# Key, value, wo and w2 loads issued from GpSimd with each engine's eight rows framed as one packet, landings relayed by the sync engine

## The chip, the cores and the metric

The kernel runs on one core of one Trainium2 chip. Its time is device microseconds of one execution of the program, here the median of several runs; a separate view of it is the profile, which records one execution instruction by instruction. The core has five engines that run their own instruction streams: TensorE (PE, with its weight loads shown as PEld), VectorE (DVE), ScalarE (ACT), GpSimd (POOL) and SyncE (SP), which computes nothing and issues transfers. Transfers between the chip's memory and the core's SBUF run on 16 DMA engines. Engines and transfers are ordered by semaphores alone.

## What is computed

One step of decoding for one token, with float32 throughout. A row x of 512 numbers is normalized; the result goes through an attention over a stored cache and through a two-layer MLP, and both are added to x:

```python
xn = _layernorm(x)                             # (1, 1, 512)
q  = (xn @ wq)                                 # 32 query heads of 128
scores = einsum(q, k) * 128 ** -0.5            # 8 key/value heads, 65536 positions, 4 queries a head
o  = softmax(scores) @ v
y  = x + o @ wo + maximum(xn @ w1, 0) @ w2     # w1: 512 x 1792, w2: 1792 x 512
```

The keys and the values are 256 MB each; wq and wo are 8 MB each, w1 and w2 3.5 MB each. Every byte is used once.

## The kernel before

All key/value heads are laid out one behind the other as 524288 positions, cut into `NCH` = 32 chunks of 16384 positions, four to a head. A chunk of keys is 8 MB and fills the tile `kt`, 128 partitions with 64 KB each; a chunk of values fills `vt` in the same way. There is one buffer of each. While keys arrive in `kt`, the values in `vt` are used, and the other way round. A third large tile, `wt`, holds w1 at first and w2 at the end. `kt` holds wq before the first keys and wo after the last.

**Who loads.** SP issues every load, in an order written out by hand: wq in three pieces (L151, L159), w1 (L160), then in turn a chunk of keys and a chunk of values (L162 to L169), then wo in three pieces (L173), w2 in five (L177) and the store of the result (L179). All go to one queue, so each DMA engine works them off in that order. Before a load into a tile that is in use, SP waits for a semaphore that says that the tile is free: `kfree` for `kt`, `vfree` for `vt`. `take` (L50) is this wait; it lowers the semaphore again. A landed load adds 16 to its own semaphore, `k` or `v`, for which PE waits in the same way (L308, L287). A partition's row of a load, 64 KB of a chunk, is one contiguous piece; an engine gets eight rows of the 128.

**What a chunk goes through.** When a chunk of keys has landed, PE multiplies it with the queries (L313) into PSUM in eight rounds, and DVE transposes the scores into the tile `tr` (L366). DVE takes the maximum (L384 to L391), and ACT computes the correction for the running maximum (L254), which adds to `kfree`, and then the exponentials (L256). When the values of the chunk have landed, PE multiplies them with the exponentials (L292); the matmul behind that (L299) adds to `vfree`. PE's loop, the block "turns", does in each turn the values of the chunk before and the keys of the next one.

**What GpSimd does.** It prepares constants (L191 to L206), the end of the normalization (L208 to L214), and then the first layer of the MLP: it waits for w1 (L217), scales w1 in place by the normalized row in four instructions (L219) and adds the four parts in three (L222 to L224). The last of them adds to `sum`, on which PE waits at L286 in the first turn that has values, ahead of those values, to add up the partitions (L281, three times, only the last of which is read). At the very end GpSimd applies the maximum with zero (L226, tile `hT`) when DVE has transposed the sums (L404, semaphore `hx`).

**The first and the last part.** wq is used like a chunk of keys with the normalized row as the query. A DVE instruction near its end, the `nop` at L365, adds to `kfree`, and the first keys may come. At the end PE multiplies wo with the heads' outputs (L313 again), w2 with `hT` (L331, L339), DVE turns the result into one row per partition (L417), and SP stores it.

Of the kernel before, what the change touches and what calls it, by code (L numbers as in the profile page):

```python
# [13 lines left out]
D = 512  # L14
# [21 lines left out]
NCH = SK // CHUNK  # L36
# [6 lines left out]
WO_CUTS = [16, 8, 8]  # L43
W2_CUTS = [6, 4, 2, 1, 1]
# [5 lines left out]
def take(e, sem, n=1):  # L50

    return e.sem_inc(sem, -n).wait_op(sem, n, "sem-ge")  # L52


def starts(cuts):
    return [sum(cuts[:i]) for i in range(len(cuts) + 1)]

# [2 lines left out]
def attention_and_mlp_kernel(  # L60
# [12 lines left out]
    sp, pe, dve, act, pool = nc.sync, nc.tensor, nc.vector, nc.scalar, nc.gpsimd  # L73
    scale = float(DH) ** -0.5

    def sbuf(name, *shape):
        return nc.alloc_sbuf_tensor(name, list(shape), F32).ap()
# [3 lines left out]
    def sem(name):  # L81
        if name not in sems:
            sems[name] = nc.alloc_semaphore(name)
        return sems[name]

    def after(ins, name, n=1):

        return ins.wait_op(sem(name), n, "sem-ge")

    kt = sbuf("kt", P, CHUNK)  # L90
    vt = sbuf("vt", P, CHUNK)
    wt = sbuf("wt", P, FB * D)
# [20 lines left out]
    hT = sbuf("hT", P, FB)  # L113
# [25 lines left out]
    wo_row = wo[0].rearrange("d j n -> d (j n)")  # L139
    w1_row = w1.rearrange("p a f -> p (a f)")  # L140
    w2_row = w2.rearrange("p b n -> p (b n)")
    v_row = v[0].rearrange("(n p b) d -> n p (b d)", p=P, b=NB)
    wq_at, wo_at, w2_at = starts(WQ_CUTS), starts(WO_CUTS), starts(W2_CUTS)

    def of_own_row(cols, groups):
# [11 lines left out]
    for i in range(1, len(WQ_CUTS)):  # L157
        cut = slice(wq_at[i], wq_at[i + 1])
        sp.dma_start(kt[:, cut], wq_row[:, cut]).then_inc(sem(WQ_SEMS[i]), 16)  # L159
    sp.dma_start(wt, w1_row).then_inc(sem("w1"), 16)  # L160
    take(sp, sem("kfree"))
    sp.dma_start(kt, k[0, 0]).then_inc(sem("k"), 16)  # L162
    with sp.Fori(0, NCH - 1) as n:
        take(sp, sem("vfree"))
        sp.dma_start(vt, v_row[bass.ds(n, 1)].rearrange("o p n -> (o p) n")).then_inc(sem("v"), 16)
        take(sp, sem("kfree"))
        sp.dma_start(kt, k[0, bass.ds(n + 1, 1)].rearrange("o p n -> (o p) n")).then_inc(sem("k"), 16)
    take(sp, sem("vfree"))
    sp.dma_start(vt, v_row[NCH - 1]).then_inc(sem("v"), 16)  # L169
    take(sp, sem("kfree"))  # L170
    for i in range(len(WO_CUTS)):
        cut = slice(wo_at[i] * D, wo_at[i + 1] * D)
        sp.dma_start(kt[:, cut], wo_row[:, cut]).then_inc(sem(f"wo{i}" if i else "k"), 16)  # L173
    sp.wait_ge(sem("hT"), 1)
    for i in range(len(W2_CUTS)):
        cut = slice(w2_at[i] * D, w2_at[i + 1] * D)
        sp.dma_start(wt[:, cut], w2_row[:, cut]).then_inc(sem(f"w2{i}"), 16)  # L177
    sp.wait_ge(sem("y"), 1)
    sp.dma_start(out.rearrange("(p a) -> p a", p=P), ysb[:, 0, :]).then_inc(sem("ends"), 16)  # L179

# [3 lines left out]
    def link(ins):  # L184

        if chain[0]:
            after(ins, "pool", chain[0])
        chain[0] += 1
        return ins.then_inc(sem("pool"), 1)
# [22 lines left out]
    link(pool.tensor_scalar_mul(xn, xc, st[:, 7:8]))  # L212
    take(pool, sem("ends"), 16)
    after(pool.tensor_copy(qpad[:, :XA], xn), "pool", chain[0]).then_inc(sem("q"), 1)  # L214
    f = DFF_ALL
    w1_of = [wt[:, a * f : (a + 1) * f] for a in range(XA)]
    pool.wait_ge(sem("w1"), 16)  # L217
# [2 lines left out]
    last.then_inc(sem("pool"), 1)  # L220
    chain[0] += 1
    after(pool.tensor_add(w1_of[0], w1_of[0], w1_of[1]), "pool", chain[0])  # L222
    link(pool.tensor_add(w1_of[2], w1_of[2], w1_of[3]))  # L223
    after(pool.tensor_add(w1_of[0], w1_of[0], w1_of[2]), "pool", chain[0]).then_inc(sem("sum"), 1)  # L224
    hbig = ysum[:, : FB * 32].rearrange("p (b i) -> p b i", i=32)
    after(pool.tensor_scalar_max(hT, hbig[:, :, 0], 0.0), "hx").then_inc(sem("hT"), 1)  # L226


    def next_of(ins):
# [41 lines left out]
    with nc.body("turns", valid_engines=[pe.engine]):  # L271
# [3 lines left out]
        with pe.If(t > 1):  # L275
# [12 lines left out]
            n = NB // WIDE  # L288
# [167 lines left out]
```

## Time and profile before

| | |
|---|---|
| time, median of 3 runs | 1303.71 us (1303.1 to 1303.74) |
| span of the profiled execution, from its first to its last instruction | 1301.3 us |
| what lies around the span, by the median | 2.4 us |
| keys: issue to landing, median of 32 | 24.1 us |
| values: issue to landing, median of 32 | 29.3 us |
| mean granted TensorE clock | 0.755 |

The profile's page shows the busy time of each engine, the span in 40 slices with the busy tenths of each engine and of the 16 DMA engines, the DMA queues with their packets, the chain of work that ended last, and the costliest groups of instructions with the idle time before them and what ended it. In a group, `out<-in` names the tiles, `x32` is the number of instructions, and L313 is line 313 of the kernel. In the timeline a row begins with its start and its duration in us; SPq and POOLq are the parts of SP and GpSimd that issue transfers and handle semaphores. A row of the busy time by windows gives the window, its length, the busy time of PE, PEld, DVE, ACT and POOL in it with the number of instructions, the granted TensorE clock, the mean busy share of the DMA engines, and GB/s.

### The profile page before, as it was taken

The numbers are of one execution on the slowest core, as the hardware profiler recorded it, in microseconds if no ns is written. First come the engines' busy times: TensorE is split into PE (matmuls) and PEld (weight loads), VectorE is DVE, ScalarE is ACT, GpSimd is POOL, SyncE is SP. The second block draws the span as 40 slices with busy tenths as digits, with TensorE's granted clock in tenths as the row PEclk, the third lists the DMA queues.
The fourth block names the chain that finished last, engine by engine and source line by source line (L and its number), as shares of the span: only waits on it lengthen the run. The fifth ranks groups of instructions, "written<-read, shape, count | busy, mean of one in ns | idle before, by whom it ended". The sixth has DMA issues, their size and how long they took to land.

```text
span 1301.3 us, 13055 instructions
## 1 busy us (share of the span) xinstructions
PE 774.9 (60%) x5474; PEld 231.1 (18%) x5474; DVE 274.8 (21%) x466; ACT 76.2 (6%) x299; POOL 34.8 (3%) x30
## 2 busy tenths in 40 slices
PE   3365674665576456566555566666567466557557
PEld 1111121111121111121111121111112111112112
DVE  2211222211222220222220122221122221122222
ACT  1000000000000000000000000000000000000000
POOL 1900000000000000000000000000000000000000
PEclk9677877776887777786776777677777777777779
DMA  9999999999999999999999999999999999999998
GB/s 403 451 419 451 419 451 419 435 435 419 451 419 451 419 451 419 449 421 423 447 419 451 419 451 419 451 419 435 435 419 451 419 451 419 451 419 443 427 420 370
DMA packets 11236, 561.02 MB, mean 431 GB/s; under 512 B 1505, under 2 KB 1505, under 8 KB 1890
## 3 DMA queue, kind: packets, MB, share of 16 engines
q1 hardware_dynamic: 11088, 561.00, 99.7%
q10 hardware_dynamic: 146, 0.00, 0.0%
q8 instruction: 1, 0.02, 0.0%
q14 instruction: 1, 0.01, 0.0%
HBM read 560.99 MB, written 0.00 MB: 431 GB/s over the span
## 4 chain that ended last, share of the span: by engine, by line
issue 94%; DMA 3%; POOL 2%; SPq 0%; PE 0%; DVE 0%; POOLq 0%
DMA wt<-w 3%; POOL wt L219 1%; POOL wt L224 0%; POOL wt L222 0%; POOL wt L223 0%; SPq L177 0%; SPq L159 0%; PE banks L339 0%; DVE ysb L417 0%; SPq L151 0%; POOL hT L226 0%; SPq L452 0%; POOLq L156 0%
## 5 line engine op out<-in xcount | busy, mean ns | idle before, releaser
L313 PE MATMUL banks<-kt,qpad 128*32 128x512 f32 x2176 | 310.0, 733 | 311.1 <-PEq L52 308.7
L292 PE MATMUL banks<-vt,probs 128*16 128x512 f32 x2048 | 271.3, 690 | 82.1 <-PEq L52 82.1
L366 DVE STREAM_TRANSPOSE tr<-banks 128x1024 f32<-128x1024 f32 x136 | 170.0, 1250 | 471.4 <-PE banks L313 466.8
L313 PEld LDWEIGHTS banks<-kt,qpad 128*32 128x32 f32 x2176 | 84.5, 131 | 509.6 <-issue 496.3
L281 PE MATMUL banks<-wt,ones 128*1 128x448 f32 x768 | 121.3, 786 | 0.0
L292 PEld LDWEIGHTS banks<-vt,probs 128*16 128x16 f32 x2048 | 68.4, 108 | 298.4 <-issue 298.4
L392 DVE COPY o_sb<-banks 128x512 f32<-128x512 f32 x32 | 22.1, 692 | 455.3 <-PE banks L292 455.3
L254 ACT ACTIVATE corr<-diff 128x8 f32<-128x8 f32 x32 | 6.7, 208 | 1179.8 <-ACTq L52 1179.8
L256 ACT ACTIVATE probs<-tr,nb_new 128x128 f32<-128x128 f32 x128 | 65.3, 521 | 0.0
L276 PE MATMUL banks<-ident,m 128*4 128x128 f32 x32 | 9.7, 303 | 78.9 <-DVE m L384 78.9
L302 PE MATMUL banks<-sel,o_sb 128*128 128x4 f32 x256 | 32.8, 252 | 18.7 <-PEq L52 18.7
L302 PEld LDWEIGHTS banks<-sel,o_sb 128*128 128x128 f32 x256 | 31.0, 191 | 20.6 <-issue 20.6
L226 POOL TENSOR_SCALAR hT<-ysum 128x14 f32<-128x14 f32 x1 | 0.3, 257 | 1220.7 <-DVE ysum L404 1220.7
L384 DVE TENSOR_REDUCE m<-tr 128x4 f32<-128x512 f32 x32 | 32.2, 1006 | 2.9
L281 PEld LDWEIGHTS banks<-wt,ones 128*1 128x1 f32 x768 | 20.2, 100 | 58.9 <-issue 58.4
L277 PE MATMUL banks<-dg,ones 4*128 4x4 f32 x64 | 15.4, 309 | 20.0 <-DVE dg L387 20.0
L256 ACT ACTIVATION_READ_ACCUMULATOR probs<-tr,nb_new 128x1 f32 x128 | 24.0, 187 | 0.0
L276 PEld LDWEIGHTS banks<-ident,m 128*4 128x4 f32 x32 | 2.6, 81 | 108.0 <-DVE m L384 108.0
L219 POOL TENSOR_SCALAR wt<-wt,xn 128x1792 f32<-128x1792 f32 x4 | 19.1, 4797 | 16.5 <-DMA wt<-w 16.5
L277 PEld LDWEIGHTS banks<-dg,ones 4*128 4x128 f32 x64 | 12.6, 245 | 27.1 <-DVE dg L387 27.1
L299 PEld LDWEIGHTS banks<-part_sum,ones 128*128 128x128 f32 x64 | 9.5, 188 | 27.2 <-issue 27.2
L395 DVE TENSOR_TENSOR lo_run<-lo_run,banks 128x8 f32<-128x8 f32 x32 | 5.2, 163 | 40.0 <-DVEq L52 40.0
(69 smaller groups left out, 91.1 us busy)
## 6 DMA issues: line engine op xcount, KB each, us to landing
kt<-wq SPq DMA_DIRECT2D x2, 2048.0 KB, 9.3
kt<-wq SPq DMA_DIRECT2D x1, 4096.0 KB, 20.8
kt<-wo SPq DMA_DIRECT2D x1, 4096.0 KB, 15.5
kt<-wo SPq DMA_DIRECT2D x2, 2048.0 KB, 22.2
wt<-w SPq DMA_DIRECT2D x1, 3584.0 KB, 28.9
wt<-w SPq DMA_DIRECT2D x1, 1536.0 KB, 9.5
wt<-w SPq DMA_DIRECT2D x1, 1024.0 KB, 11.7
kt<-k SPq DMA_DIRECT2D x32, 24.1
```

The lines of the kernel that those rows point to most:

```text
L219: last = pool.tensor_scalar_mul(w1_of[a], w1_of[a], xn[:, a : a + 1])
L256: last = act.activation(probs[:, :, g], tr[:, :, g], AF.Exp, bias=nb_new[:, g : g + 1], scale=scale, accum_out=part_sum[:, g : g + 1],)
L276: after(pe.transpose(pma[:GROUP, :P], m, ident), "d2p").then_inc(sem("p2d"), 1)
L277: after(pe.matmul(pmb[:, :GROUP], ones[:GROUP, :], dg, start=True, stop=True), "d2p", 2).then_inc(sem("p2d"), 1)
L281: ins = pe.matmul(hrow[32 * c : 32 * c + 1, :], ones[:, :1], hb[:, :, 32 * c : 32 * c + 32], start=True, stop=True,)
L292: last = pe.matmul(acc[c : c + WIDE * GROUP, :], probs[:, b : b + WIDE, :].rearrange("p b g -> p (b g)"), vt[:, b * DH : (b + WIDE) * DH], ...
L299: pe.matmul(lo_new[:, 0, :], ones, part_sum, start=True, stop=True).then_inc(sem("vfree"), 1)
L302: last = pe.matmul(lo_new[:, 1, :], o_sb[:, b, :], sel[:, b, :], start=(b == 0), stop=(b == WIDE - 1),)
L313: last = pe.matmul(pair[s // 2 % 2][32 * c : 32 * c + 32, s % 2 * 512 : s % 2 * 512 + 512], qpad, kb[:, s * 16 : s * 16 + 16, c, :], start ...
L366: ins = after(dve.transpose(tr2[:, s * 1024 : (s + 1) * 1024], pair[s % 2]), "p2d", s + 1)
L384: dve.reduce_max(m, tr.rearrange("p b i -> p i b")[:, :GROUP, :], axis=AX.X).then_inc(sem("d2p"), 1)
L392: after(dve.tensor_copy(o_sb.rearrange("p b d -> p (b d)"), acc), "p2d", 7).then_inc(sem("d2p"), 1)
```

## The change

Five things are done.

- SP no longer issues keys, values, wo and w2. GpSimd does, in `load_keys`, `load_values` and two loops, each with the same wait for `kfree`, `vfree` or `hT` as before. GpSimd has a queue of its own for them; wq, w1 and the store stay on SP's.
- Each of these loads, but for the first chunk of keys, is issued with `single_packet=True`: the eight rows that a DMA engine gets of it are framed as one packet.
- The landings of keys and values count up two new semaphores, `k_in` and `v_in`, which nothing lowers. SP waits for each landing in turn and adds 16 to `k` or `v` (`relay`), on which PE waits as before. The first piece of wo is passed on in the same way.
- The first keys and the first values are issued by GpSimd between its copy of the normalized row (L214) and its wait for w1 (L217). The second chunk of keys and all that follow stand behind its work on w1 (L224).
- w2 is issued by GpSimd behind its own instruction that writes `hT`.

```diff
+def relay_of(sem):
+
+    def relay(e, to, of, n):
+        e.sem_inc(sem(to), 16).wait_op(sem(of), n, "sem-ge")
+
+    return relay
...
-    take(sp, sem("kfree"))
-    sp.dma_start(kt, k[0, 0]).then_inc(sem("k"), 16)
-    with sp.Fori(0, NCH - 1) as n:
-        take(sp, sem("vfree"))
-        sp.dma_start(vt, v_row[bass.ds(n, 1)].rearrange("o p n -> (o p) n")).then_inc(sem("v"), 16)
-        take(sp, sem("kfree"))
-        sp.dma_start(kt, k[0, bass.ds(n + 1, 1)].rearrange("o p n -> (o p) n")).then_inc(sem("k"), 16)
-    take(sp, sem("vfree"))
-    sp.dma_start(vt, v_row[NCH - 1]).then_inc(sem("v"), 16)
-    take(sp, sem("kfree"))
-    for i in range(len(WO_CUTS)):
-        cut = slice(wo_at[i] * D, wo_at[i + 1] * D)
-        sp.dma_start(kt[:, cut], wo_row[:, cut]).then_inc(sem(f"wo{i}" if i else "k"), 16)
-    sp.wait_ge(sem("hT"), 1)
-    for i in range(len(W2_CUTS)):
-        cut = slice(w2_at[i] * D, w2_at[i + 1] * D)
-        sp.dma_start(wt[:, cut], w2_row[:, cut]).then_inc(sem(f"w2{i}"), 16)
+    for n in range(NCH):
+        relay(sp, "k", "k_in", 16 * (n + 1))
+        relay(sp, "v", "v_in", 16 * (n + 1))
+    relay(sp, "k", "wo0", 16)
     sp.wait_ge(sem("y"), 1)
...
     after(pool.tensor_copy(qpad[:, :XA], xn), "pool", chain[0]).then_inc(sem("q"), 1)
+    def load_keys(n, **how):
+        take(pool, sem("kfree"))
+        pool.dma_start(kt, k[0, n], **how).then_inc(sem("k_in"), 16)
+
+    def load_values(n):
+        take(pool, sem("vfree"))
+        pool.dma_start(vt, v_row[n], single_packet=True).then_inc(sem("v_in"), 16)
+
+    load_keys(0)
+    load_values(0)
...
     after(pool.tensor_add(w1_of[0], w1_of[0], w1_of[2]), "pool", chain[0]).then_inc(sem("sum"), 1)
+    for n in range(1, NCH):
+        load_keys(n, single_packet=True)
+        load_values(n)
+    take(pool, sem("kfree"))
+    for i in range(len(WO_CUTS)):
+        cut = slice(wo_at[i] * D, wo_at[i + 1] * D)
+        pool.dma_start(kt[:, cut], wo_row[:, cut], single_packet=True).then_inc(sem(f"wo{i}"), 16)
     hbig = ysum[:, : FB * 32].rearrange("p (b i) -> p b i", i=32)
     after(pool.tensor_scalar_max(hT, hbig[:, :, 0], 0.0), "hx").then_inc(sem("hT"), 1)
+    pool.wait_ge(sem("hT"), 1)
+    for i in range(len(W2_CUTS)):
+        cut = slice(w2_at[i] * D, w2_at[i + 1] * D)
+        pool.dma_start(wt[:, cut], w2_row[:, cut], single_packet=True).then_inc(sem(f"w2{i}"), 16)
```

More of the change, by code (lines that the diff above doesn't have):

```diff
@@ L88, in after @@
         return ins.wait_op(sem(name), n, "sem-ge")
+    relay = relay_of(sem)
     kt = sbuf("kt", P, CHUNK)
```

## The prediction

> **What bounds the kernel now.** I read the page from the top: the span, the busy shares, the DMA row of the 40 slices, the queues, the chain.
>
> ```profile
> span 1301.3 us, 13055 instructions
> PE 774.9 (60%) x5474; PEld 231.1 (18%) x5474; DVE 274.8 (21%) x466; ACT 76.2 (6%) x299; POOL 34.8 (3%) x30
> ...
> DMA  9999999999999999999999999999999999999998
> GB/s 403 451 419 451 419 451 419 435 435 419 451 419 451 419 451 419 449 421 423 447 419 451 419 451 419 451 419 435 435 419 451 419 451 419 451 419 443 427 420 370
> DMA packets 11236, 561.02 MB, mean 431 GB/s; under 512 B 1505, under 2 KB 1505, under 8 KB 1890
> ...
> q1 hardware_dynamic: 11088, 561.00, 99.7%
> ...
> issue 94%; DMA 3%; POOL 2%; SPq 0%; PE 0%; DVE 0%; POOLq 0%
> ```
>
> No engine is busy over 60%, while the 16 DMA engines are at nine tenths or more in every slice but the last. The chain calls 94% "issue" because it cannot follow a semaphore loop back to a transfer, so the DMA row decides: all 561 MB come through SP's queue q1. The 11088 packets of q1 are 9856 rows (128 for each of 64 key and value loads, 3 of wq, 1 of w1, 3 of wo, 5 of w2, and the store) and 16 semaphore writes for each of these 77 transfers (1232): **every row is a packet of its own.**
>
> Does a gap or the rate make the 1301 us? In the busy time by windows the last two columns are the DMA share and GB/s, and a packet is booked where it starts. Narrow windows therefore give the duration of one packet (share x width x 16 engines), and windows around a burst give the cadence.
>
> ```profile
> 608.42:608.43 0.01, 0.01 (x4) 0.00 (x0) 0.00 (x0) 0.01 (x1) 0.00 (x0) 0.50 15.12 6554
> 1284.36:1284.38 0.02, 0.02 (x4) 0.00 (x0) 0.00 (x0) 0.00 (x0) 0.00 (x0) 1.00 1.91 819
> 1292.54:1292.56 0.02, 0.00 (x0) 0.00 (x0) 0.02 (x1) 0.00 (x0) 0.00 (x0) 1.00 0.97 410
> 1294.66:1294.68 0.02, 0.02 (x3) 0.02 (x1) 0.00 (x0) 0.00 (x0) 0.00 (x0) 1.00 0.50 205
> ```
>
> ```profile
> 610.83:611.21 0.38, 0.15 (x4) 0.00 (x0) 0.00 (x0) 0.00 (x0) 0.00 (x0) 0.50 6.39 2760
> 1249.38:1249.87 0.49, 0.00 (x0) 0.00 (x0) 0.00 (x0) 0.00 (x0) 0.00 (x0) 0.50 4.96 2140
> ```
>
> The first row is one packet of 64 KB (6554 GB/s x 0.01 us): 15.12 x 0.01 x 16 = 2.419 us. The others are 16, 8 and 4 KB: 0.611, 0.310 and 0.160 us. The second pair each hold 16 rows of 64 KB, the first row on each engine of the key load issued at 607.56 and of the last value load, 33 loads on: (1249.62 - 611.02) / 33 = 19.35 us a load, which is 8 x 2.419. So there is **no gap between loads**: 64 x 19.35 = 1238 us of the span are packets end to end. The durations are a straight line plus a constant: from 4 to 64 KB, (2.419 - 0.160) / 60 = 0.03765 us per KB, so 64 KB are 2.410 us and 9 ns are left over; 16 KB gives 8.5 ns, 8 KB 9 ns. Each row costs **9 ns beside its bytes**. That, and the start and the end, is all that an issue can win.
>
> **The change, part by part.** *Framing.* 31 key loads (the first is not framed), 32 value loads, 3 of wo and 5 of w2 become one packet per engine: 71 loads with seven packet ends fewer each. The trace has no packet of several rows. If the 9 ns go with the packet, 7 x 9 = 63 ns a load and 71 x 63 ns = 4.5 us go; if they go with the row, nothing; the bytes alone set 2.410 us a row, so more cannot go and nothing in these rows makes it a loss. I take 4.5: in every row above the constant comes with one packet end, from 4 to 64 KB alike.
>
> By the Trainium skill (DMA: Bandwidth & Descriptors, Why small descriptors are slow) a packet costs about 3 cycles inside the engine, joining descriptors saves only that and is "only worth it at ≤256 B desc size", which speaks against this change. At that page's 850 MHz that is 3.5 ns of the 9 measured, by estimate 71 x 7 x 3.5 ns = 1.7 us.
>
> *Issue from GpSimd in the stream.* A load must have its first packet ready when the one before it ends.
>
> ```profile
> 607.56 0.33 SPq L167 DMA_DIRECT2D kt<-k  x1
> 621.20 0.33 SPq L165 DMA_DIRECT2D vt<-v  x1
> ...
> 0.73 0.39 SPq L151 DMA_DIRECT2D kt<-wq  x1
> ...
> 1298.92 0.34 SPq L179 DMA_DIRECT2D y<-ysb  x1
> ```
>
> ```profile
> 2.04:2.08 0.04, 0.00 (x0) 0.00 (x0) 0.00 (x0) 0.04 (x1) 0.04 (x1) 1.00 1.82 410
> 1299.74:1299.78 0.04, 0.00 (x0) 0.00 (x0) 0.00 (x0) 0.00 (x0) 0.00 (x0) 1.00 0.11 4
> ```
>
> The key load issued at 607.56 starts near 611.1: 3.5 us of cover. The rows that group all issues, from the page and from the view of the keys' line, say how it stands to the others (the last figure is us from issue to landing):
>
> ```profile
> kt<-k SPq DMA_DIRECT2D x32, 24.1
> vt<-v SPq DMA_DIRECT2D x32, 29.3
> ```
>
> ```profile
> DMA to landing us min/median/max: 23.5/24.1/25.3
> ```
>
> Less 19.35 us of transfer, the keys have 4.1 to 6 us and the values some 10, with the way to the landing's semaphore in it; laying the 19.35 us grid over the issue times gives the keys in steady turn 3.5, 4.0 and 4.9 us. An issue on SP takes 0.84 us to the first packet at the end (1298.92 to 1299.76) and 1.3 us at the start (0.73 to 2.06). The trace has no load issued by GpSimd. Its nearest rows are its own small instructions:
>
> ```profile
> 2.92 0.52 POOL L206 MEMSET x<- 128x512 f32 x1
> ...
> 65.02 0.21 ACT L254 ACTIVATE corr<-diff 128x8 f32<-128x8 f32 x1 [50.54 <-ACTq L52]
> ...
> 65.47 0.34 SPq L167 DMA_DIRECT2D kt<-k  x1
> ```
>
> So I bound it by 0.84 us from below and by 1.3 + 0.52, near 1.9 us, from above, and take 1.6; the far end would be the 4.8 us of a 128x1792 instruction of GpSimd (its row is below), far more elements than a few hundred descriptors. The added relay on SP costs one hop, at most the 0.24 us from the end of the ACT instruction that frees kt (65.23) to SP's issue (65.47), and every matmul on a new load starts that much later. Behind a waiting relay on SP stand only later relays and the store, in the order in which loads land. 3.5 - 0.24 leaves 3.3 us against 1.6: **hidden, cost nothing.** Without cover it would be 31 key loads' excess. SP's loop with its registers goes; nothing waited for it.
>
> The Trainium skill (same page, Specifications) gives about 1 us to the first byte from GpSimd and 0.6 from SP; no run here shows the first yet.
>
> *The start.* This is where the move costs. GpSimd now issues K0 and V0 at the first kfree, then scales and sums w1, and only then issues K1.
>
> ```profile
> 26.46 0.33 SPq L162 DMA_DIRECT2D kt<-k  x1
> ...
> 31.17 19.12 POOL L219 TENSOR_SCALAR wt<-wt,xn 128x1792 f32<-128x1792 f32 x4 [16.46 <-DMA wt<-w]
> ...
> 58.39 3.99 POOL L224 TENSOR_TENSOR wt<-wt 128x1792 f32<-128x1792 f32 x1
> ...
> 64.23 4.66 PE L281 MATMUL banks<-wt,ones 128*1 128x448 f32 x24
> 69.91 7.06 PE L292 MATMUL banks<-vt,probs 128*16 128x512 f32 x64 [1.02 <-PEq L52]
> ```
>
> ```profile
> 28.15:28.62 0.47, 0.00 (x0) 0.00 (x0) 0.13 (x2) 0.00 (x0) 0.00 (x0) 0.72 2.27 976
> 29.20:29.68 0.48, 0.00 (x0) 0.00 (x0) 0.00 (x0) 0.00 (x0) 0.00 (x0) 0.50 2.22 956
> 30.32:30.74 0.42, 0.00 (x0) 0.00 (x0) 0.00 (x0) 0.00 (x0) 0.00 (x0) 0.50 5.82 2497
> ```
>
> On one queue K0 stood behind w1: the last two rows of w1 (16 of 28 KB each) start near 28.4 and 29.4, K0's near 30.5, w1 is used from 31.17 and its work ends at 62.4, 31.2 us later. On a queue of its own K0's first row is ready near 28.1 and can get in between. How two queues share an engine the trace does not show: from no row of K0 ahead of what is left of w1 (two rows and the semaphore write) to one ahead of each of the three, 0 to 3 x 2.42 us. I take two, 4.8 us: w1 is used from 36.0, its work ends at 67.2, K1's first packet is ready at 68.8. V0 ends at 30.5 + 2 x 19.35 = 69.2. Hidden by 0.4 us; three rows give 71.2, **2.0 us of empty queues, once.** The bytes of K0 and w1 together are the same, so K0 does not land later. PE needs the sum for L281, so V0's matmuls move from 69.9 to about 72; vfree follows near 79.5 where it was 77.5, and the cover of V1's load was 11 us: hidden.
>
> *The end.* wo is issued as the keys were. w2 is issued behind hT:
>
> ```profile
> 1283.09 0.26 POOL L226 TENSOR_SCALAR hT<-ysum 128x14 f32<-128x14 f32 x1 [1220.72 <-DVE ysum L404]
> 1283.38 2.24 SPq L177 DMA_DIRECT2D wt<-w  x5
> ...
> 1288.22:1288.26 0.04, 0.00 (x0) 0.00 (x0) 0.00 (x0) 0.00 (x0) 0.00 (x0) 1.00 0.74 307
> ```
>
> Its first row starts at 1288.24, 4.9 us after hT; GpSimd's 1.6 us for the first fit, and the others have the time of the transfers before them. Cost nothing. PE waits for w2 directly, with no relay. Of the relays the one for wo0 is hidden, as PE is then still on the last values.
>
> *Sum*: 1301.3 - 4.5 = 1296.8 us of span; 2.4 us lie around it (1303.7 median less 1301.3), left as they are: **1299.2 us**.
>
> **Rivals.**
> 1. *The 9 ns belong to the row, or mostly.* For it: the semaphore write is a packet too, and 8 x 2.419 leaves no room for its 9 ns in 19.35, so a packet end by itself may be cheap. Then nothing goes, 1303.7; with three eighths of it gone, 1302.0. Chance 0.24. By the skill's 3 cycles it would be this 1302.0.
> 2. *K0 keeps the engines ahead of w1* (slower). If an engine that has begun K0 takes all its rows before it returns to w1, w1 lands 8 x 2.42 = 19.4 us later, its work ends at 81.8, K1 is ready at 83.4 where V0 ended at 69.2: 14.2 us of empty queues, 1313.4. It outweighs the framing once w1's work ends 4.5 us past the point of no gap (67.6), at 72.1: more than four rows of K0 ahead. Against it: rows are packets on SP's queue, and K0 is the one load left unframed. Chance 0.10.
> 3. *GpSimd issues too slowly.* From 3.3 us to the first packet on, a third of the key loads come late. At 3.7 us the gain is gone (31 / 3 x 0.4 = 4.1), at 5 us it is 31 x (1.7 + 1.2 + 0.3) / 3 = 33 us, 1332. For it: nothing here shows that price; against it: 1.9 from the nearest rows. Chance 0.09.
> 4. *Three rows ahead of w1*: the forecast and 2.0 us, 1301.2. Chance 0.07.
>
> That the change does not do what it says would look like the first rival: rows still packets of 2.419 us.
>
> **How the numbers follow.** The forecast, 1299.2, has 0.50: framing takes the whole constant and both moves are hidden. A measurement of this kernel can tell about 0.2%, 2.6 us, from no change: faster is below 1301.1, slower above 1306.3. Faster: 0.50. Within: rivals 1 and 4, 0.31. Slower: rivals 2 and 3, 0.19. The range begins 0.8 us below the forecast (9.5 ns for 9 are 0.25 us, the runs of before differ by 0.6), covers rivals 4 and 1, and ends at 1306.0, a little overrun of rival 3 without its body; what it leaves out is the rest of rivals 2 and 3.
>
> **What will show it.** Framing: the burst windows 33 loads apart, 19.29 us a load and not 19.35. Issue: the same cadence with no break, and GpSimd's issue to landing near the 24 us of keys before. Start: the first use of w1 near 36 us (31 if none is ahead, 50 for rival 2), and K1's first packet near 69. I am wrong if the cadence stays at 19.35 or rises, or if a slice of the DMA row after the first drops below nine tenths.

## The result: 13.0 us slower, half in the stream and half behind the store

The changed kernel takes **1316.37 us** (median of 4 runs, 1314.29 to 1319.97) against 1303.4 (1302.9 to 1303.74) for the kernel before on the same chip: ratio 1.0102, 95% interval 1.0086 to 1.0118. The forecast was 1299.2, with a range up to 1306.0. The profiled execution took 1315.45 us, of which the span is 1313.5.

The lines of the profile's page that answer to those of before:

```profile
span 1313.5 us, 12900 instructions
...
DMA  9999999999999999999999999999999999999996
...
q0 software_dynamic: 10240, 548.93, 97.0%
q1 hardware_dynamic: 720, 12.06, 2.2%
...
kt<-k POOLq DMA_DIRECT2D x32, 24.3
```

The DMA engines are still at nine tenths everywhere but at the end, so no slice shows a hole: the loss must be mostly in rows that last longer, and in the last slice, which has gone from 8 to 6. The move itself was made (549 MB by GpSimd's queue q0). Packets are still booked row by row: 72 loads of 128 rows and 16 semaphore writes are 10368, and 256 packets of 2 KB, the last pieces of w2, are booked as 128 of 4 KB; the kernel without framing, below, has the same 10240.

Where do the 12.2 us of span come from? In the busy time by windows of the kernel after, the last two columns are DMA share and GB/s; each of these windows holds one row of 64 KB for each of the 16 engines, the first rows of K1 and, 59 loads on, of V30.

```profile
69.16:70.36 1.20, 0.00 (x0) 0.00 (x0) 0.00 (x0) 0.00 (x0) 0.00 (x0) 1.00 2.02 874
1216.34:1217.78 1.44, 0.00 (x0) 0.00 (x0) 0.00 (x0) 0.00 (x0) 0.00 (x0) 0.50 1.69 728
```

(1217.06 - 69.76) / 59 = **19.45 us a load** where it was 19.35: over the 62 loads from K1 to wo some 6 us. And the 16 engines no longer step together: their first rows start within 1.2 to 1.4 us of each other, where they did within 0.4 to 0.5 (the windows ahead of the forecast).

The end, in the timeline of the kernel after, then in the group view of its last line (times in ns, then from and to in us):

```profile
1305.33 0.35 SPq L176 DMA_DIRECT2D y<-ysb  x1
```

```profile
L470 POOLq DRAIN  x3: 40/78/5946, 1306.9 to 1313.3; - x3
```

The same group in the kernel before:

```profile
L452 POOLq DRAIN  x3: 34/46/64, 1300.4 to 1301.1; - x3
```

The store is issued 6.4 us later than before (1298.92). That is the stream, with 0.3 us from the start. From the store to the end of the span are 8.2 us where there were 2.4, and **one instruction makes up the 5.8 us: GpSimd's drain at the kernel's end lasts 5946 ns instead of 64.** The waits of SP in the two kernels name only TensorE's side of the last barrier:

```profile
SPq L470 <- PEq L470: 6.6, 2, 6.2
```

```profile
SPq L452 <- PEq L452: 1.5, 2, 1.1
```

All engines sit in that barrier until GpSimd has drained. Sum: 0.3 + 6.0 + 0.1 + 5.8 = 12.2 us.

Where in the stream? At the key loads. K9 of the kernel after, in the timeline of POOL and in windows of 0.02 us (share x 0.02 x 16 is the duration of the rows that start in a window, here one each):

```profile
378.79 0.53 POOL L214 DMA_DIRECT2D kt<-k  x1 [24.05 <-POOLq L52]
```

```profile
378.84:378.86 0.02, 0.02 (x8) 0.00 (x0) 0.00 (x0) 0.02 (x1) 0.02 (x1) 0.50 7.56 3277
380.00:380.02 0.02, 0.02 (x4) 0.00 (x0) 0.00 (x0) 0.02 (x1) 0.00 (x0) 0.50 10.11 3277
380.26:380.28 0.02, 0.02 (x8) 0.02 (x4) 0.00 (x0) 0.00 (x0) 0.00 (x0) 0.50 10.58 3277
381.00:381.02 0.02, 0.02 (x8) 0.00 (x0) 0.00 (x0) 0.00 (x0) 0.00 (x0) 0.50 7.58 3277
```

A row at 378.84, of the load before, lasts the usual 2.42 us. Rows that engines begin 1.2 and 1.5 us after the issue of K9 last 3.24 and 3.39 us; one begun 2.2 us after it lasts 2.43. So an engine that reaches a load too soon after its issue is mostly not idle by the record, it has a **stretched row**: the DMA line of the slices cannot show it. The queues' shares say how much of this there is: 97.0% and 2.2% of 1313.5 us are 1303 us of packets for each engine, where 99.7% of 1301.3 were 1297. Longer packets make up some 5.6 us (a share is rounded to 0.1%, which is 1.3 us). Added up one by one in the two traces, the packets are 1298.0 and 1303.1 us for each engine, 5.1 us more, of which 4.2 lie in the first rows of K1 to K31; the last 1.1 us are engines that wait between two rows (0.02 us in the kernel before).

### The profile page after: what moved, and what is told of

Its sections match the earlier page's. It is cut to its first block, busy times and chain, and to the rows that moved or that the text cites. A ratio compares the mean times of both kernels' runs of the same rounds, so it can differ in the third digit from the quotient of the medians.

```text
span 1313.5 us, 12900 instructions
## 1 busy us (share of the span) xinstructions
PE 772.1 (59%) x5474; PEld 230.7 (18%) x5474; DVE 274.8 (21%) x466; ACT 76.2 (6%) x299; POOL 73.2 (6%) x102
## 5 line engine op out<-in xcount | busy, mean ns | idle before, releaser
L310 PE MATMUL banks<-vt,probs 128*16 128x512 f32 x2048 | 275.1, 698 | 90.2 <-PEq L52 90.2
L299 PE MATMUL banks<-wt,ones 128*1 128x448 f32 x768 | 117.6, 765 | 0.0
L214 POOL DMA_DIRECT2D kt<-k x32 | 17.2, 536 | 735.4 <-POOLq L52 735.4
L218 POOL DMA_DIRECT2D vt<-v x32 | 16.9, 529 | 429.8 <-POOLq L52 429.8
```

Of the source, the lines that this page charges most:

```text
L214: pool.dma_start(kt, k[0, n], **how).then_inc(sem("k_in"), 16)
L218: pool.dma_start(vt, v_row[n], single_packet=True).then_inc(sem("v_in"), 16)
L299: ins = pe.matmul(hrow[32 * c : 32 * c + 1, :], ones[:, :1], hb[:, :, 32 * c : 32 * c + 32], start=True, stop=True,)
L310: last = pe.matmul(acc[c : c + WIDE * GROUP, :], probs[:, b : b + WIDE, :].rearrange("p b g -> p (b g)"), vt[:, b * DH : (b + WIDE) * DH], ...
```

## The experiments

Theory: two costs, unconnected. The stream's 6 us come from too little cover (the time from the issue of a key load to the first engine's first row), the 5.8 us from the number of loads that GpSimd issued. Rivals: the framing stretches the rows; GpSimd's issue is slow in itself, whatever the cover; the relay; the engines put out of step at the start by two queues. Ratios are to the kernel before on the same chip, with 95% intervals.

### Is it the framing?

**e1**, after without framing:

```diff
-        pool.dma_start(vt, v_row[n], single_packet=True).then_inc(sem("v_in"), 16)
+        pool.dma_start(vt, v_row[n]).then_inc(sem("v_in"), 16)
...
-        load_keys(n, single_packet=True)
+        load_keys(n)
```

(wo and w2 likewise.)

> The changed kernel with no load framed; GpSimd still issues. If the framing makes the stream slower (an engine must have a whole packet of eight rows before it goes on), the 6.1 us that the stream lost between the first rows of the second keys (69.48 us) and of wo (1275.27 us) go and the time is about 1310 us; if it is GpSimd's issue that comes too close to the end of the load before, they stay and the time is about 1316 us. Either way the last DRAIN of GpSimd keeps its 5.9 us, and a row of 64 KB its 2.419 us.

Measured: 1318.81 us (ratio 1.0111, 1.0096 to 1.0127), beside the 1.0102 of the kernel after: the intervals overlap. The stretched rows and the 5946 ns stay. The framing is not the cause of the loss.

**e2** gives the key buffer free some 4 us earlier, from VectorE after the transposes of the scores; **e3** is e2 without framing.

```diff
-        act.activation(corr, diff.unsqueeze(1).to_broadcast([P, 2, GROUP]), AF.Exp).then_inc(sem("kfree"), 1)
+        act.activation(corr, diff.unsqueeze(1).to_broadcast([P, 2, GROUP]), AF.Exp)
...
-            turn_scores()
+            turn_scores(free="kfree")
```

> The changed kernel, framed, with kt freed when the last score matmul has read it (by the DVE nop ahead of the last transpose, as for wq) and not by ACT some 5 us later, so that the key loads are issued some 5 us earlier. If too little cover stretches the first rows of key loads, the stream is back at 19.35 to 19.37 us a load, and the time is about 1310 us (5.9 us of drain left). If framing or the software queue as such stretches them, nothing changes: about 1316 us.

> The early release of kt and no framing. With the cover theory and with the framing theory about 1310 us, with a software queue that is slower as such about 1316 us. Beside the framed one with the early release it shows what framing is worth when nothing is late: 0 us if the 9 ns belong to the row, 4.5 us if they belong to the packet.

Measured: e2 1310.15 us (1.0054, 1.004 to 1.0067), e3 1309.93 (1.0051, 1.0037 to 1.0065). In e2 the first rows of K1 and, 61 loads on, of V31:

```profile
69.02:70.12 1.10, 0.00 (x0) 0.00 (x0) 0.00 (x0) 0.00 (x0) 0.00 (x0) 0.50 2.21 953
1249.34:1250.52 1.18, 0.00 (x0) 0.00 (x0) 0.00 (x0) 0.00 (x0) 0.00 (x0) 0.50 2.06 889
```

(1249.93 - 69.57) / 61 = 19.35 us a load: with 7.6 us of cover the stream is that of before, and the 1.1 us between engines do no harm. What is left is the drain (5946 ns as in after) and 0.7 us until the store, which is issued at 1299.58. And in this undisturbed stream framing gains nothing: 71 x 63 ns would be 4.5 us, 0.2 were measured, and the step is 8 x 2.419 as before. The Trainium skill (DMA: Bandwidth & Descriptors, Why small descriptors are slow) holds joining worth it only up to 256 bytes; these rows have 65536, and the runs agree with it. That its 3 cycles a packet would go, as the estimate beside the forecast had it (1.7 us), these two runs do not show: the framed one is not the faster.

### How much cover, and is it GpSimd alone?

**e14** is the kernel after with the release some 1.4 us earlier; **e12** is the kernel before with the release of e2; **e5** and **e6** give the release *later* by 1.4 us, with ACT's third exponential, in before and in after.

```diff
 e14, behind the maximum's diagonal (dg) on VectorE; ACT's release goes
+            dve.nop().then_inc(sem("kfree"), 1)
 e5 and e6, in ACT's loop of exponentials; the release at corr goes
+            if g == 2:
+                last.then_inc(sem("kfree"), 1)
```

> After, with the release of the key buffer given about 1.4 us earlier in the chunk than ScalarE gives it, so that GpSimd's lead on the first engine's first row goes from 2.0 us to some 3.4 us. If the stream's 6 us come from cover that is too small by about a microsecond, the first rows last as in the rest of the stream, the loads take 19.35 us, and the time is 1309.5 to 1310.5, as with the release at 6.7 to 8.7 us; what stays over before is the wait at the kernel's end. If they come from GpSimd's issue in itself, whatever the cover, 1316 stays; if the cover is still short for part of the engines, 1311 to 1315.

> The kernel before with the early release of kt: SP issues the keys some 5 us earlier. It had the cover that its issue needs (0.01 us of stretch a load) and its queue never ran empty, so within 0.5 us of 1303.4. If there was hidden stretch in it, up to 2 us less.

> The kernel before with kfree given 1.4 us later (by ACT's third exponential and not by the correction ahead of the four), so that SP issues the keys with some 2 to 3.5 us of cover and not 3.5 to 5. If only GpSimd's issue needs more than that, nothing changes: within 0.5 us of 1303.3. If any load issued that close to the end of the one before stretches its first rows, 3 to 10 us more.

> The same delay in the changed kernel. If its 6.1 us come from too little cover for GpSimd's issue, each of the 31 key loads loses about as much more as it has less cover: 1316.4 + 20 to 45 us, about 1335 to 1360. If the framing or the software queue as such stretched the rows, about 1316 as it was.

Measured: e14 1309.55 us (1.0045, 1.0031 to 1.0059), e12 1303.46 (0.9999, 0.999 to 1.0008), e5 1313.86 (1.0084, 1.007 to 1.0097), e6 1335.35 (1.0252, 1.0236 to 1.0267). In e14, K2's issue in the timeline and the first rows of K1 and of V30, 59 loads on:

```profile
101.54 0.53 POOL L214 DMA_DIRECT2D kt<-k  x1 [20.47 <-POOLq L52]
```

```profile
68.96:69.56 0.60, 0.00 (x0) 0.00 (x0) 0.00 (x0) 0.00 (x0) 0.00 (x0) 0.50 4.05 1748
1210.65:1211.59 0.94, 0.00 (x0) 0.00 (x0) 0.00 (x0) 0.00 (x0) 0.00 (x0) 0.50 2.58 1116
```

(1211.12 - 69.26) / 59 = 19.35: **a release some 1.4 us earlier brings the whole stream back**, with GpSimd issuing and the loads framed. The mean cover of K1 to K31 even goes from 2.6 us to 5.1, as the engines also step closer again (their first rows within 0.8 us in the mean, 1.7 in after). And e5 shows that SP's queue does the same when its cover is short. In e5 K4 is issued by SP at 185.89; a first row 1 us later, and one 2.5 us later:

```profile
185.89 0.33 SPq L167 DMA_DIRECT2D kt<-k  x1
```

```profile
186.88:186.90 0.02, 0.02 (x8) 0.00 (x0) 0.00 (x0) 0.00 (x0) 0.00 (x0) 0.50 10.31 3277
188.36:188.38 0.02, 0.00 (x0) 0.00 (x0) 0.00 (x0) 0.00 (x0) 0.00 (x0) 0.50 7.58 3277
```

10.31 is 3.30 us, 7.58 is 2.43. The same 1.4 us later cost before 10 us and after another 19. So the stretch is not GpSimd's; before had 3.3 to 5.2 us of cover, which is enough (e12, with more, is not faster), but not much more than enough.

### What took the cover?

**e7** and **e8** measure an issue by itself: the release is moved behind the chunk's last copy (`o_sb`), in before and in after, so that every key load is issued into an empty queue. Each was run once, with a profile.

```diff
-        act.activation(corr, diff.unsqueeze(1).to_broadcast([P, 2, GROUP]), AF.Exp).then_inc(sem("kfree"), 1)
+        act.activation(corr, diff.unsqueeze(1).to_broadcast([P, 2, GROUP]), AF.Exp)
...
             after(dve.tensor_copy(o_sb.rearrange("p b d -> p (b d)"), acc), "p2d", 7).then_inc(sem("d2p"), 1)
+            dve.nop().then_inc(sem("kfree"), 1)
```

> The kernel before with kfree given only behind the copy of o_sb, so that a key load is issued into an empty queue, some 10 us after the values landed: what SP's issue takes to the first row of each engine is seen by itself. About 0.9 to 1.3 us to the first and less than 0.5 us between the first and the last engine. Each chunk costs 11 to 13 us more: about 1303 + 31 x 12 = 1675 us.

> The same in the changed kernel: GpSimd's issue into an empty queue. The cover theory needs 2 us or more to the first engine and up to 4 us to the last, or first rows that last longer than 2.42 us; if it is as quick as SP's, within 0.5 us, the theory falls. The time is that of the one before and 31 x 1 to 2 us, and the drain.

Measured: 1698.11 and 1708.52 us. One issue of SP in e7, and the rows behind it (6554 GB/s are two rows of 64 KB in 0.02 us, 3277 one):

```profile
638.44 0.33 SPq L167 DMA_DIRECT2D kt<-k  x1
```

```profile
639.38:639.40 0.02, 0.02 (x2) 0.02 (x2) 0.00 (x0) 0.00 (x0) 0.00 (x0) 1.00 0.00 0
639.40:639.42 0.02, 0.02 (x2) 0.02 (x1) 0.00 (x0) 0.00 (x0) 0.00 (x0) 1.00 19.35 6554
639.52:639.54 0.02, 0.02 (x2) 0.02 (x2) 0.00 (x0) 0.00 (x0) 0.00 (x0) 1.00 21.44 6554
640.38:640.40 0.02, 0.00 (x0) 0.00 (x0) 0.00 (x0) 0.00 (x0) 0.00 (x0) 0.50 7.61 3277
```

One of GpSimd in e8:

```profile
642.05 0.53 POOL L214 DMA_DIRECT2D kt<-k  x1 [50.09 <-POOLq L52]
```

```profile
643.26:643.28 0.02, 0.02 (x1) 0.00 (x0) 0.00 (x0) 0.00 (x0) 0.00 (x0) 1.00 0.00 0
643.28:643.30 0.02, 0.02 (x1) 0.00 (x0) 0.00 (x0) 0.00 (x0) 0.00 (x0) 1.00 9.47 3277
643.48:643.50 0.02, 0.00 (x0) 0.00 (x0) 0.02 (x1) 0.00 (x0) 0.00 (x0) 1.00 11.00 3277
644.12:644.14 0.02, 0.00 (x0) 0.00 (x0) 0.02 (x1) 0.00 (x0) 0.00 (x0) 1.00 7.78 3277
```

From issue to first packet SP takes 0.96 us and GpSimd 1.23. The Trainium skill (DMA: Bandwidth & Descriptors, Specifications) has 0.6 and 1 us to the first byte; here the instruction's own time is in it, and the order agrees. But in the windows shown the early first rows last 3.03 to 3.52 us with GpSimd (9.47 and 11.00 x 0.32) and 3.10 to 3.43 with SP: a row is as late as if it had begun at full rate up to 2.5 us after GpSimd's issue (643.48 + 3.52 - 2.42 = 644.58), and up to 2.1 after SP's (639.52 + 3.43 - 2.42 = 640.53). Over 30 key loads of each run this time is, from the first to the last engine and in the mean, 1.8 to 2.5 us for GpSimd and 1.6 to 2.2 for SP. That is the cover that a load needs; between the two engines it differs by only some 0.3 us.

The expectation of e8 had two signs, and both came: GpSimd is as quick to the first packet as SP within 0.5 us, which speaks against an issue that is slow in itself, and the first rows last longer than 2.42 us, but with SP too. Its time is 10.4 us above that of e7, where 31 to 62 us and the drain had been expected; beside the 5.9 us of the drain that is 0.15 us a load.

The rest is in the timeline of the turn of K1, first of after, then of before (the matmuls on K1; the correction that frees the buffer; the issue of K2):

```profile
90.25 9.79 PE L331 MATMUL banks<-kt,qpad 128*32 128x512 f32 x64 [8.67 <-PEq L52]
...
104.76 0.21 ACT L272 ACTIVATE corr<-diff 128x8 f32<-128x8 f32 x1 [37.72 <-ACTq L52]
...
105.55 0.53 POOL L214 DMA_DIRECT2D kt<-k  x1 [24.43 <-POOLq L52]
```

```profile
89.25 9.01 PE L313 MATMUL banks<-kt,qpad 128*32 128x512 f32 x64 [10.36 <-PEq L52]
...
102.73 0.21 ACT L254 ACTIVATE corr<-diff 128x8 f32<-128x8 f32 x1 [35.51 <-ACTq L52]
...
103.18 0.33 SPq L167 DMA_DIRECT2D kt<-k  x1
```

GpSimd starts its issue 0.58 us after ACT's instruction (104.97 to 105.55), SP 0.24 (102.94 to 103.18): 0.34 us. TensorE begins K1 1.0 us later: the load is in when the *last* engine is done, and the last one began K1 at 70.34 where it was 69.36. That is the whole 1.0, so the relay by SP is hardly in it. The rest is the length of TensorE's pass, which varies from turn to turn in both kernels. K2 has 2.3 us of cover left, and its rows begin to stretch.

The mean of K1 to K31 is free of that luck. Their cover is 2.6 us (1.2 to 3.6) in after and 4.1 us (3.3 to 5.2) in before. Of that, 0.35 us go with GpSimd's later start, the same in every turn, and 1.4 with the engines: their first rows lie 1.7 us apart where they lay 0.4. Some 0.2 us come back, as the chunk's work up to the release was a little shorter. The relay takes nothing: TensorE begins 0.55 us after the end of a load's last row in after, and 0.60 in before. What first parts the engines, by 0.9 us at K0 and 1.2 at K1, these runs do not show.

**e13** is before with the relay alone, by ACT; **e11** is after with K0 and V0 issued by SP behind w1 on its queue, and GpSimd from K1 on, so that no second queue disturbs the start. K1 and V1 also wait for a semaphore `go`, which SP raises when K0 and V0 have landed (left out of the lines below).

```diff
 e13
+        take(act, sem("k_in"), 16)
+        act.sem_inc(sem("k"), 16)
 e11, on SP; load_keys(0) and load_values(0) of GpSimd go
+    take(sp, sem("kfree"))
+    sp.dma_start(kt, k[0, 0]).then_inc(sem("k_first"), 16)
+    take(sp, sem("vfree"))
+    sp.dma_start(vt, v_row[0]).then_inc(sem("v_first"), 16)
```

> Before with one part alone: the sync engine still issues every load, but a landing of keys and of values reaches TensorE through an instruction of ScalarE, which takes the DMA's semaphore and passes it on. If the passing on does not touch the cover of the key loads (it lies behind the landing, and the release comes from ScalarE as before), 1303.4 within 1 us, and the first rows of the key loads last as in before. If the passing on takes the cover by itself, the first rows of K1 to K30 stretch as in the kernel after, and the time is 1306 to 1316.

> The changed kernel, framed and with the late release of kt, in which SP issues the first keys and the first values, behind w1 on its own queue as before, and GpSimd all loads from the second keys on. If the changed kernel fell below the needed cover because its first keys, issued on a second queue 3.1 us before w1 was through, put the 16 engines 1 to 2 us apart, they stay within 0.5 us of each other here, the stream is at 19.35 us a load and the time about 1310 us (the drain is left). If GpSimd's later start and the relay take the cover away by themselves, the stream still loses 3 to 6 us: 1313 to 1316 us.

Measured: e13 1303.5 us (1.0003, 0.9994 to 1.0012); the cover of K1 to K31 is 3.96 us in the mean where before has 4.13. The relay alone, here by ScalarE, takes under 0.2 us and costs nothing. e11 1317.19 (1.0096, 1.0081 to 1.0111): K1 has 2.5 us of cover there, its first rows are stretched by 0.46 us per engine, and the engines, 0.5 us apart at K0, are 2.9 apart at K1 (15 of them 0.9) and stay 1.2 to 3.0 apart. **So two queues at the start are not needed for the fall**: it sets itself off, once the cover is near 2.5 us. Whether they play a part in after e11 leaves open, since its K1 was issued later (66.34, and 65.60 in after) and had 2.5 us of cover where that of after has 3.6.

### What makes the wait at the end?

**e4** (before with one small load, `xrow` of 2 KB, by GpSimd), **e10** (before with the 5 loads of w2 by GpSimd), **e9** (e2 with 32 loads by GpSimd, the rest by SP).

```diff
 e4
+    pool.dma_start(xrow, x.rearrange("(o n) -> o n", o=1)).then_inc(sem("xrow"), 16)
-    act.dma_start(xrow, x.rearrange("(o n) -> o n", o=1)).then_inc(sem("xrow"), 16)
 e10
-        sp.dma_start(wt[:, cut], w2_row[:, cut]).then_inc(sem(f"w2{i}"), 16)
+        pool.dma_start(wt[:, cut], w2_row[:, cut]).then_inc(sem(f"w2{i}"), 16)
 e9, on GpSimd; SP issues the rest as in before
-    for n in range(1, NCH):
+    for n in range(1, NCH // 2):
```

> The kernel before with one load, the 2 KB of xrow, issued by GpSimd and not by ACT; everything else is SP's. If the 5.9 us drain of GpSimd at the end is a price for having issued any load, the time is 1303.4 + 5.8, about 1309.2 us; if the drain grows with the number of loads (72 in the changed kernel), it is within 0.3 us of 1303.4. The stream should keep 19.35 us a load in both cases.

> The kernel before in which GpSimd issues w2 alone (5 loads, unframed), behind hT. A drain that grows with the loads is 64 + 5 x 82 = 0.5 us and the time 1303.3 + 0.4 and up to 0.5 for a later issue of w2, 1303.7 to 1304.2 us; a drain that is a step with large loads, or one that lasts from the last load issued, is 5.9 us and the time 1309 us.

> The kernel of the early release, in which GpSimd issues the first 16 chunks (32 loads) and SP the other 16, wo and w2. If the drain of GpSimd at the end grows by some 80 ns a load (5946 ns with 72 loads, 133 with one, 64 with none), it is 2.7 us here and the time about 1303.3 + 2.8 + what the change of queues in the middle costs once (0 to 5 us); if it is a step that any large load sets off, 5.9 us.

Measured: 1303.32 us (1.0001, 0.9992 to 1.001), 1304.41 (1.0012, 1.0003 to 1.0021) and 1307.41 (1.0029, 1.0017 to 1.0041). The drains of e4, e10 and e9:

```profile
L452 POOLq DRAIN  x3: 40/71/133, 1300.9 to 1301.5; - x3
```

```profile
L452 POOLq DRAIN  x3: 40/78/469, 1301.1 to 1301.9; - x3
```

```profile
L479 POOLq DRAIN  x3: 40/78/2679, 1302.5 to 1305.6; - x3
```

With 0, 1, 5, 32 and 72 loads the longest drain is 64, 133, 469, 2679 and 5946 ns: **60 ns and 82 ns for each load** that GpSimd has issued. It goes by loads, not by bytes: the 2 KB of e4 cost 69 ns, the loads of e9, of 8 MB, 82. In e11, where SP issues two of the 72, it is 5782 ns, 2 x 82 less. In e9 another 1.3 us went, most of it at the hand-over, where SP issued its first load of values 1 us before its first row (668.66 to 669.62). e10 lies 0.2 us above its expectation: five of its 11 runs took 1305.7 to 1307.0 us, and why is not known, as the one with a trace took 1304.27.

Can this be done earlier? **e15** is e14 (1309.55 us) with a drain of GpSimd behind its last issue of w2; **e16** has it behind wo, ahead of hT.

```diff
 e15, behind the loop that issues w2 (e16: behind the one that issues wo)
+    pool.drain()
```

> The kernel with the release 1.4 us earlier (1309.55), and a drain of GpSimd behind its last issue of w2, some 15 us before the result is stored. If the wait at the end is work that GpSimd owes for each load that it has issued, and that any drain works off, the added drain takes it beside the last transfers, the one at the end falls from 5946 ns to about 0.1, and the time is 1303.4 to 1304.2, that of the kernel before. If the drain at the end costs its 82 ns a load whatever came before it, it stays at 5946 ns and the time at 1309.5; if the added drain waits for w2 to land, part of it is left and the time lies between.

> The same with the added drain behind the issue of wo, ahead of the first layer's maximum (hT), so that 67 of GpSimd's 72 loads lie before it and the 5 of w2 behind it. If a drain works off what is owed so far, the one at the end is that of the run with w2 alone, about 470 ns, and the time 1303.8 to 1304.6, unless the added drain waits for wo to land and holds hT and with it the issue of w2 back: then the last transfers start later and the time is above 1304.6. If the drain at the end costs for every load, 5946 ns and 1309.5 stay.

Measured: e15 1305.38 us (1.0014, 1.0005 to 1.0023), e16 1312.82 (1.0069, 1.0055 to 1.0083). The two drains of e15, by the group views of their lines:

```profile
L245 POOLq DRAIN  x1: 15862/15862/15862, 1285.8 to 1285.8; - x1
```

```profile
L472 POOLq DRAIN  x3: 34/46/77, 1303.1 to 1303.6; - x3
```

It is work that is owed, and any drain does it: the last one is down to 77 ns, and 4.2 us are back. The added one ends at 1301.6, though, 3.5 us after the last packet of w2 (1298.2): it also waits for loads in flight, which leaves 1.8 us over before. In e16, for the same reason (the added drain ends at 1292.5, 3.2 us after the last packet of wo), hT comes at 1292.6 and not at 1283.5 as in e15, and w2's transfer starts late; the drain at the end has the 472 ns of five loads. How a drain shares its time between waiting and working off is not settled by these two runs.

## Why the prediction was wrong

- **What bounds the kernel** was right: the transfers, end to end. That only an issue's cost could be won was right too, and there was less to win than thought.
- **"71 x 63 ns = 4.5 us go" failed.** The 9 ns beside a row's bytes are the row's: e2 and e3, the same stream framed and unframed, differ by 0.2 us. This is rival 1 in full, which had 0.24. The constant was read rightly from four sizes, but in each of them one row was one packet, so nothing in those rows told the two apart; it should not have been the likeliest case. Whether a framed load is one packet inside the engine the trace does not tell, since it books rows.
- **"3.5 - 0.24 leaves 3.3 us against 1.6: hidden, cost nothing" failed**, and cost 6 us. The first packet came sooner than 1.6 (1.23 in e8). But the first packet's start was the wrong point: its row is late until 1.8 to 2.5 us after the issue. And 3.3 was the wrong cover: the 3.5 that it began with was read to the middle of the 16 engines (611.02) and not to the first of them (610.84). From it the forecast took off one hop of 0.24 and left out that GpSimd starts 0.34 us later than SP, and that a load is in only when the last of 16 engines is, with engines that no longer step together. 2.3 us were left at K2. Rival 3 named this place, but looked for a slow issue; a small one was enough, as less is hidden than the mean shows.
- **"2.4 us lie around it, left as they are" and the span's end, "Cost nothing", failed by 5.8 us.** The issue of w2 was hidden as forecast; what GpSimd owes for all 72 loads falls due at the end, and no step of the forecast had it. The trace of before had its drain of 64 ns, with no load issued by GpSimd to grow it.
- **The start was right in its result and not in its working.** "I take two, 4.8 us": no row of K0 got ahead of w1, and w1 is used from 31.19, as before (31.17). Rivals 2 and 4 did not occur. The first rows of K1 start 0.3 us later. The row of after:

```profile
31.19 19.12 POOL L226 TENSOR_SCALAR wt<-wt,xn 128x1792 f32<-128x1792 f32 x4 [2.82 <-DMA wt<-w]
```

Of the 17.2 us between forecast and result, 4.5 are the framing, 6 the stream, 5.8 the drain and 0.3 the start; the rest is the difference of one profiled execution from the median.

## What to carry to other kernels

Measure the cover of a load from its issue to the *first* engine that is free for it, in the worst turn, and hold it against the time until its rows run at full rate, not until the first packet: here some 2.5 us. A stream with 1 us to spare stands still at its rate and falls off when about that much goes, on SP's queue as on GpSimd's, while the busy share goes on showing nine tenths. Before moving many loads to an engine, look at what the engine owes for each at the kernel's end, and whether a drain in an earlier pause can pay it.

## What the runs showed of the hardware that was not expected

- A drain of GpSimd takes about 82 ns for each load that it has issued since the last drain (5946 ns for 72). The Trainium skill (VectorE: DVE Perf Modes, The DRAIN you can't avoid) calls the drains at a kernel's two ends boilerplate of about 12 ns, constant on all five engines; SP's three take 7 ns here, and GpSimd's longest is no constant.
- The DMA engines of one core drift apart, by up to 2.8 us in after (K8), when first rows are stretched. In e2, where none is from K1 on, they keep their distance: 1.1 us at K1 and at K31.
- Single rows of 64 KB last the same 2.419 us, with the 9 ns in it, whether their load is framed or not.
